# One DMA transpose moved behind the repeat copies, filler matmuls on vacated row tiles, and two of the last stores on the GpSimd queue

## The chip, the cores and the metric

The kernel runs on one core of a Trainium2 chip. The metric is the device time in microseconds (us) of one execution; a group of unprofiled runs is summed up by its median. One further execution was recorded by the hardware profiler, and all rows shown come from that execution. The engines are TensorE (PE in the rows, with its weight loads as PEld), VectorE (DVE), ScalarE (ACT), GpSimd (POOL) and SyncE (SP). DMA transfers are issued from the queues of SP, ACT and POOL.

## The reference, cut to what matters

Two layers follow each other: an attention over 32 inducing points, and a feed-forward layer with a parametric ReLU.

```
x: (4, 12480, 128)   inducing: (32, 128)   w_in: (128, 2048)   w_out: (2048, 128)   alpha: (2048)

mab(q, kv) = softmax(q @ kv.T / sqrt(128)) @ kv
h   = mab(inducing, x)                 # (4, 32, 128): one small summary for each batch
a   = mab(x, h)                        # (4, 12480, 128)
y   = a.reshape(49920, 128) @ w_in     # (49920, 2048)
g   = max(y, 0) + alpha * min(y, 0)
out = g @ w_out                        # (49920, 128), float32
```

Since `a` is a softmax over 32 rows of `h`, the kernel never forms it: `y` is the 32 exponentials of a token times the small matrix `h @ w_in` (32 x 2048), and the softmax's division is left to the very end. With g = relu(y) * (1 - alpha) + alpha * y, the second term is linear and also becomes a 32 x 128 matrix.

## The kernel before, in words

**Work units.** A batch has 12480 tokens: six supers of 2048 tokens (index `u` or `s` from 0 to 5) and a remainder of 192 tokens (index 6, `NS`). A super has four groups of 512 tokens, so a batch has groups `g` = 0 to 24, of which 24 is the remainder. A group's hidden layer has 16 chunks of 128 features (`KC`).

**First pass of a batch, over x.** `a_load` (line 170) loads a super of x through the POOL queue, cast to bf16, into `xn`. `a_xpose` (line 188) makes its transpose `xT` by one DMA transpose on the SP queue. `t_scores` and `t_accum` (lines 403, 417) or, for later batches, `a_scores` and `a_accum` then add to the summary `h`. This pass of batch `b + 1` runs during the second pass of batch `b`. In the second batch (batch 1) the supers 0 and 1 are transposed on PE, and the remainder and the supers 2 to 5 by DMA.

**Second pass of a batch, over its groups.** For each super `b_scores` (487) makes the exponentials `e` and writes them to DRAM scratch `e2d`; `b_rep` (511) reads them back four times, once into each quarter of the partitions, with four DMAs on the SP queue: the tile `rep`. `b_den` and `b_turn` (534, 552) write the reciprocals of the softmax's sums to scratch `rt` and read them back four times as `rdT`, also on SP. "The weights' copies" in the change's name are these `rdT` and `rep` transfers: the softmax weights of a super, copied to four places.

Then for each group:

- `fill` (595): a 32-row matmul on one of PE's four row tiles (`f` = 0 to 3; rows 32f to 32f+31) from `rep` and `hW` into a PSUM bank, and a ReLU by ACT (line 613) or DVE (616) into `gt`;
- `piece` (620): a 32-row matmul of `gt` with the weights `W1`, added up in the group's own bank; all 16 chunks times four row tiles must be added;
- `finish` (652): a DVE transpose of the finished bank (663), a multiply by `rdT` on POOL (666), and four stores of a quarter each (680).

**The planner.** `tokens` (817) writes out the order of all instructions by hand with a modelled clock (`clk`). Most groups are "laned": a group does its 16 pieces on row tile 0, then its 16 pieces on tile 1, and so on (`moving`, `tile[f]`), so that up to four groups are on the array at once, one on each row tile. A matmul on a free tile is a `fill` of a chunk needed later. The three last groups of the last batch, 22, 23 and 24, are not laned: their chunks are filled during the laned stage, and after it each is added with 128-row matmuls (`linear_whole`, `whole`; the `tail` loop at line 1071). When the laned stage starts, tiles 2 and 3 have no group yet, and `warm` matmuls, whose result is not used, run there into banks taken for that purpose (`fresh`, lines 949, 993, 1036).

**Tasks.** `at(t, ...)` (844) ties other work to the start of the t-th laned group (`T0` = 9 is the first of them). Tasks with the same t run in the order in which `at` was called; those of the current batch's second pass are entered before those of the next batch's first pass. `cross` (878) holds the t at which each super of batch 1 is given to `a_xpose`, in the order 0, 1, remainder, 2, 3, 4, 5. At `T0 + 6` stand the `rt` and `e2d` writes of batch 0 and the transpose of super 4; at `T0 + 7` stand `b_turn` (four `rdT` reads) and `b_rep` (four `rep` reads); at `T0 + 8` the transpose of super 5, whose x load is a task of `T0 + 6`.

**Stores.** They go to the POOL queue, except for the last four groups (`ending`, line 677): group 21's four go to SP, and those of groups 22 to 24 alternate between SP and ACT. Each DMA of the SP and ACT queues is given one of eight completion semaphores in turn, and its issue waits until the former DMA with that semaphore has landed; the POOL queue has eight of its own.

Of the kernel before, what the change touches and what calls it, by code (L numbers as in the profile page):

```python
# [41 lines left out]
def kernel(  # L42
# [9 lines left out]
    nc = tc.nc  # L52
# [3 lines left out]
    B, N, C = x.shape  # L56
# [8 lines left out]
    NG = NS * NQ + 1  # L65
# [7 lines left out]
    def pin(bi):  # L73
        ins = bi.ins
        e = ins.engine
        if e in last:
            tc.add_manual_dep(
                ins,
                last[e],
                mybir.DependencyInfo(  # L80
                    mybir.DependencyClass.NoSync, mybir.DependencyReason.DATA
                ),
                reason="program order",
            )
        last[e] = ins.name
        return bi
# [20 lines left out]
    number = {id(t): i for i, t in enumerate(banks)}  # L107
# [6 lines left out]
    clk = Clock()  # L114
    idle = list(range(NBANK - 2))

    def bank():
        i = min(idle, key=lambda i: clk.free[i])
        idle.remove(i)
        clk.pe = max(clk.pe, clk.free[i])  # L120
        return banks[i]
# [251 lines left out]
    def h_sum(st):  # L373
        st.et = work.tile([P, 1], f32, name="et", tag="et")
        pin(nc.vector.reduce_sum(out=st.et[:], in_=st.es[:], axis=AXX))
# [186 lines left out]
    def shape_of(g):  # L562
        return (P, NB, 1) if g < NS * NQ else (PR, JR, 2)
# [4 lines left out]
    begun = set()  # L568
    seen = {}
    held = []  # L570

    def units(g):
        return KC // shape_of(g)[2]

    def acc_of(b, g):
        if (b, g) not in accs:
            accs[b, g] = bank()
            left[b, g] = 4 * units(g) + 1
        return accs[b, g]
# [72 lines left out]
    def finish(b, g):  # L652
        st = states[b]
        pp, nb, _ = shape_of(g)
        t = pp * nb
        acc = acc_of(b, g)
        s, q = divmod(g, NQ)
        rq = st.rden[s][:, :, :, q : q + 1]
        rbc = bass.AP(
            tensor=rq.tensor, offset=rq.offset, ap=[rq.ap[0], rq.ap[1], rq.ap[2], [0, 32]]  # L660
        )
        ot = ot_pool.tile([P, GRP], f32, name="ot", tag="ot")
        pin(nc.vector.transpose(out=ot[:, :t], in_=acc[:, :t]))  # L663
        drained(accs[b, g], "D", 74 + t * 1.04)
        ob = ob_pool.tile([P, GRP], f32, name="ob", tag="ob")
        pin(nc.gpsimd.tensor_tensor(  # L666
            out=ob[:, :t].rearrange("p (k m c) -> p k m c", k=nb, c=32),
            in0=ot[:, :t].rearrange("p (k m c) -> p k m c", k=nb, c=32),
            in1=rbc, op=MULT,
        ))  # L670
        t0 = b * N + s * SUP
        if s < NS:
            dst = out[t0 : t0 + SUP, :].rearrange(
                "(i b q) (a k) -> q a i b k", b=t // 32, q=NQ, k=32)[q]
        else:
            dst = out[t0 : t0 + REM, :].rearrange("(i b) (a k) -> a i b k", b=t // 32, k=32)
        ending = b == B - 1 and g >= NG - 4
        for a in range(4):
            eng = (nc.sync, nc.scalar)[a % 2] if ending and g >= NG - 3 else nc.sync if ending else nc.gpsimd
            pin(eng.dma_start(  # L680
                out=dst[a],
                in_=ob[32 * a : 32 * a + 32, :t].rearrange("p (b k) -> p b k", k=32),
            ))
        st.rep.pop(g)

    order = [0, 1, NS] + list(range(2, NS))
# [3 lines left out]
    src = x[0, 0:SUP, :].rearrange("(p q j) c -> p q (j c)", q=NQ, j=NB)  # L690
# [27 lines left out]
    for q in range(4):  # L718
        sl = slice(32 * q, 32 * q + 32)
        pin(nc.gpsimd.memset(pick[sl, q : q + 1], 1.0))  # L720
        for q2 in range(4):
            pin(nc.gpsimd.tensor_copy(
                out=fold[sl, 32 * q2 : 32 * q2 + 32], in_=ident32[sl, sl]
# [93 lines left out]
    def tokens(st):  # L817
# [17 lines left out]
        need = [((first[y], 1, u), (*y, u)) for y in laned for u in range(KC)]  # L835
        need += [((c, 0, i), ch) for c, w in enumerate(wholes) for i, ch in enumerate(w)]
        need += [((len(laned) + i, 0, u), (*y, u)) for i, y in enumerate(tail) for u in range(units(y[1]))]
        need = [ch for _, ch in sorted(need)]
        SESSIONS = 8
        T0 = SESSIONS + 1  # L840
# [17 lines left out]
        for b in range(B):  # L858
            base = T0 + (first[b, 0] if b else -2)
            for s in range(1, NS + 1):  # L860
                t = base + 4 * s - AHEAD if b or s > 2 else 4 * s - 2
                nt = t + 4 if s < NS else t + 2
                at(t, lambda b=b, s=s: b_scores(states[b], s))
                at(t + 1, lambda b=b, s=s: b_rep(states[b], s))
                at(nt, lambda b=b, s=s: b_den(states[b], s))
                at(nt + 1, lambda b=b, s=s: b_turn(states[b], s))
            if b + 1 < B:
                n = b + 1
                E = base + 4 * NS
                if b:  # L870
                    lag = (-8, -4, -4, 0, 4, 8, 10) if b > 1 else (-4, 0, 0, 4, 6, 8, 10)
                    score = [base + k for k in lag]
                    load = [t - 7 for t in score]
                    cross = [t - 5 for t in score]
                else:
                    score = [T0 + k for k in (2, 4, 4, 6, 9, 11, 13)]
                    load = [0, 0, 5, SESSIONS, T0 + 2, T0 + 4, T0 + 6]
                    cross = [None, None, 6, T0 + 1, T0 + 4, T0 + 6, T0 + 8]
                    at(7, lambda: p_xpose(states[1], 0, 0))
                    at(SESSIONS, lambda: p_xpose(states[1], 0, 1))  # L880
                    at(T0 + 2, lambda: p_xpose(states[1], 1, 0))
                    at(T0 + 3, lambda: p_xpose(states[1], 1, 1))
                sums = [T0 + k for k in (4, 6, 6, 9, 11, 13, 14)] if n == 1 else [k + 4 for k in score]
                fs, fa = (t_scores, t_accum) if n == 1 else (a_scores, a_accum)
                for u, k, c, t, e in zip(order, score, cross, load, sums):
                    at(e, lambda n=n, u=u, fa=fa: fa(states[n], u))
                    at(k, lambda n=n, u=u, fs=fs: fs(states[n], u))
                    if c is not None:
                        at(c, lambda n=n, u=u: a_xpose(states[n], u))
                    at(t, lambda n=n, u=u: a_load(states[n], u, pieces=NQ if n > 1 else 2))  # L890
                H = sums[-1]
                if n == 1:
                    at(H + 1, lambda n=n: h_make(states[n]))
                    H += 2
                else:
                    at(score[-1] + 1, lambda n=n: h_sum(states[n]))
                    at(H, lambda n=n: h_den(states[n]))
                    at(H + 1, lambda n=n: h_transpose(states[n]))
                    H += 2
                assert H <= E - 6  # L900
                at(H, lambda n=n: h_weights(states[n]))
                at(H, lambda n=n: b_scores(states[n], 0))
                at(H, lambda n=n: h_linear(states[n]))
                at(H + 1, lambda n=n: b_rep(states[n], 0))
                at(E - 4, lambda n=n: b_den(states[n], 0))
                at(E - 3, lambda n=n: b_turn(states[n], 0))
                fn = lambda n=n: states.setdefault(n, new_batch(n))
                tasks.setdefault(load[0], []).insert(0, fn)
# [31 lines left out]
        queue = list(laned)  # L940
        tile = [None] * 4
        moving = []
        free_at = [clk.pe] * 4
# [5 lines left out]
        fresh = {f: bank() for f in (2, 3)}  # L949
# [10 lines left out]
        while queue or moving or any(tile):  # L960
            best = []
            taken = {q for _, q, _ in moving}
            for f in range(4):
                if tile[f]:
# [3 lines left out]
                    elif (*y, todo[0]) in seen:  # L968
                        t = max(free_at[f], seen[*y, todo[0]][1] - 100)
                        best.append((t, 1, f, "piece"))  # L970
                else:
# [4 lines left out]
                    if f == 0 and queue and lanes < LANES and (  # L976
# [3 lines left out]
                        if ch in seen:  # L980
                            t = max(free_at[f], seen[ch][1] - 100 - SLOT)
                            best.append((t, 2, f, "start"))
            if fillable():
                since = max(min(clk.free[i] for i in idle) - 40, landed.get(need[0][:2], 0))
                hungry = min(clk.act, clk.dve) < clk.pe + hungry_at
                for f in range(4):
                    t = max(free_at[f], since)
# [5 lines left out]
            for f in sorted(fresh):  # L993
                if soon and f not in taken:
                    best.append((free_at[f], 9, f, "warm"))
            assert best, (need[:2], len(seen), tile, moving, queue[:2])
            if closed:
                calm = [x for x in best if x[3] == "piece" and x[2] and x[2] not in gate]
                calm += [x for x in best if x[3] == "warm"]
                best = calm or [x for x in best if x[3] == "piece"] or best  # L1000
# [9 lines left out]
            if what == "start":  # L1010
                m = first[queue[0]]
                if pause(T0 + m):
# [8 lines left out]
                    free_at = [clk.pe] * 4  # L1021
# [4 lines left out]
            if what == "enter":  # L1026
# [4 lines left out]
                if f in fresh:  # L1031
                    i = number[id(fresh.pop(f))]
                    clk.free[i] = clk.pe + SLOT
                    idle.append(i)
                continue
            if what == "warm":
                mm(
                    fresh[f][:], W1[rows, 0, :],
                    W1[rows, 0:NB, :].rearrange("p k c -> p (k c)"), skip_group_check=True,
                )  # L1040
                free_at[f] = clk.pe + SLOT
                continue
# [23 lines left out]
                        flush()  # L1066
            free_at[f] = clk.pe + SLOT
        clk.pe = max(clk.pe, max(free_at) + SWITCH)
        for t in sorted(tasks):
            run_tasks(t)  # L1070
        for y in tail:
# [43 lines left out]
```

## Time and profile before

| | us |
|---|---|
| unprofiled runs | 563.68, 565.47, 568.73 (median 565.47) |
| the profiled execution | 570.99 |
| its span, from the first to the last instruction | 569.2 |
| mean granted TensorE clock in it | 0.988 of full speed |
| busy in the span: PE, ACT, DVE, POOL | 546.6, 505.3, 500.4, 408.7 |
| DMA queues' share of 16 engines: POOL's, SP's | 36.4%, 26.8% |
| longest idle time of PE after its start | 3.26 (from 88.66 to 91.93) |

The span is what the rows describe; the profiled execution's own time is 1.8 us longer. Times within the span are counted from its start. PE's busy time counts any moment at which at least one row tile works, so 96% does not mean that all four row tiles work.

### The profile page before, as it was taken

To read this page: it belongs to the slowest core of one execution; us is meant where nothing else is said; L and a number is where in the kernel's file an instruction comes from. 1 tells how busy PE (TensorE), PEld (TensorE's weight loads), DVE (VectorE), ACT (ScalarE), POOL (GpSimd) and SP (SyncE) were. 2 spreads that over 40 slices of the span, in tenths; PEclk is the share of its full clock that TensorE was granted. 3 is DMA by queue.
4 is the path that set the end of the run, shared out by engine and by line. 5 is a ranking of instruction groups with operands and counts; after the bars stand their busy time and mean duration, and the time that the engine had idled before them with its cause. 6 is when DMAs were issued, how large, how long until landed. Compare 5 with 4: busy or idle time off the path is not lost.

```text
span 569.2 us, 21360 instructions
## 1 busy us (share of the span) xinstructions
PE 546.6 (96%) x8860; PEld 295.4 (52%) x8864; DVE 500.4 (88%) x861; ACT 505.3 (89%) x1005; POOL 408.7 (72%) x600
## 2 busy tenths in 40 slices
PE   4999997999999999999999999999999999999995
PEld 4645553455455454454555565455555454474642
DVE  3689995899998999999999999999989999999971
ACT  2479995998999999999999999999999999999970
POOL 6646574676688997785987976865778777668681
PEclk9999997999999999999999999999999999999988
DMA  9976999555599997866796894333344244243233
GB/s 198 225 145 125 144 168 157 101 119 82 108 190 159 165 170 142 149 129 107 138 176 123 161 181 115 77 89 68 86 95 113 59 105 102 54 97 66 53 62 62
DMA packets 111201, 69.25 MB, mean 122 GB/s; under 512 B 79824, under 2 KB 101696, under 8 KB 111104
## 3 DMA queue, kind: packets, MB, share of 16 engines
q0 software_dynamic: 23280, 38.53, 36.4%
q1 hardware_dynamic: 85152, 28.52, 26.8%
q8 instruction: 69, 1.13, 0.9%
q10 hardware_dynamic: 2672, 0.84, 0.6%
q14 instruction: 28, 0.23, 0.1%
HBM read 41.00 MB, written 28.95 MB: 123 GB/s over the span
## 4 chain that ended last, share of the span: by engine, by line
POOL 35%; PE 32%; issue 20%; PEld 5%; DVE 4%; DMA 2%; POOLq 0%; SPq 0%; PEldq 0%; ACT 0%; DVEq 0%
PE bank L135 30%; POOL out_dram L680 23%; POOL ob L666 11%; PEld L135 5%; DVE gt L616 2%; PE bank L223 2%; POOL xn L177 1%; DMA ind_f<-in_inducing_dram 1%; DMA rep<-e2d 1%; DVE ot L663 1%; DVE hW L310 1%; DMA out_dram<-ob 0%; DVE xT L229 0%; POOLq L666 0%; PEldq L1061 0%
## 5 line engine op out<-in xcount | busy, mean ns | idle before, releaser
L135 PE MATMUL bank<-gt,W 32*128 32x512 bf16 (+2 forms) x6013 | 490.7, 376 | 4.3 <-issue 3.6
L613 ACT ACTIVATE gt<-bank 128x512 bf16<-128x512 f32 (+1 forms) x920 | 470.2, 615 | 23.9 <-PE bank L135 19.6
L616 DVE TENSOR_SCALAR gt<-bank 128x512 bf16<-128x512 f32 (+1 forms) x648 | 406.6, 677 | 26.8 <-PE bank L135 22.7
L135 PE MATMUL bank<-rep,hW 32*128 32x512 bf16 (+1 forms) x1600 | 415.5, 370 | 2.4 <-DVE hW L310 0.3
L135 PEld LDWEIGHTS <-W 32*128 32x128 bf16 (+1 forms) x6079 | 228.9, 92 | 188.5 <-issue 114.6
L680 POOL DMA_DIRECT2D out_dram<-ob x384 | 246.2, 672 | 43.0 <-POOL ob L666 28.9
L666 POOL TENSOR_TENSOR ob<-ot,rdT 128x512 f32<-128x512 f32 (+1 forms) x100 | 109.4, 1094 | 100.4 <-DVE ot L663 88.8
L135 PEld LDWEIGHTS <-hW 32*128 32x128 bf16 x1600 | 134.0, 92 | 36.7 <-issue 18.6
L663 DVE STREAM_TRANSPOSE ot<-bank 128x512 f32<-128x512 f32 (+1 forms) x100 | 69.7, 698 | 19.0 <-PE bank L135 18.0
L177 POOL DMA_DIRECT2D xn<-in_x_dram x70 | 40.2, 648 | 4.6 <-DMA xn<-in_x_dram 2.4
L135 PE MATMUL bank<-rep,hA 32*128 32x512 bf16 x94 | 35.3, 379 | 0.3 <-DVE hW L310 0.3
L229 DVE COPY xT<-bank 128x1024 bf16<-128x1024 bf16 (+1 forms) x16 | 10.7, 672 | 4.7 <-PE bank L223 4.6
L250 ACT ACTIVATE e1t<-bank 128x256 bf16<-128x256 f32 (+1 forms) x13 | 4.8, 371 | 9.9 <-PE bank L135 8.7
L135 PEld LDWEIGHTS <-hA 32*128 32x128 bf16 x94 | 8.5, 91 | 7.1 <-issue 5.3
L223 PE MATMUL bank<-ident,xn 128*128 128x128 bf16 x128 | 11.3, 242 | 0.9 <-DVE xn L781 0.9
L135 PE MATMUL bank<-xT,hT 128*32 128x512 bf16 (+1 forms) x98 | 10.4, 389 | 0.4 <-ACT gt L613 0.4
L135 PE MATMUL bank<-W 32*128 32x512 bf16 x63 | 10.3, 376 | 0.0
L498 ACT ACTIVATE e<-bank,rs 128x512 bf16<-128x512 f32 x12 | 8.5, 708 | 1.8 <-PE bank L135 1.7
L223 PEld LDWEIGHTS <-xn 128*128 128x128 bf16 x128 | 8.7, 109 | 2.1 <-DVE xn L781 1.0
L498 ACT ACTIVATE e<-bank 128x512 bf16<-128x512 f32 x12 | 7.5, 626 | 1.9 <-PE bank L135 1.8
L135 PE MATMUL bank<-IT,xT 128*128 128x32 bf16 x192 | 8.0, 179 | 0.6 <-issue 0.4
L135 PEld LDWEIGHTS <-e 128*128 128x128 bf16 x96 | 4.3, 96 | 7.4 <-issue 7.4
(100 smaller groups left out, 145.4 us busy)
## 6 DMA issues: line engine op xcount, KB each, us to landing
out_dram<-ob POOLq DMA_DIRECT2D x372, 64.0 KB, 2.7
rep<-e2d SPq DMA_DIRECT2D x92, 128.0 KB, 3.6
xn<-in_x_dram POOLq DMA_DIRECT2D x48, 128.0 KB, 5.8
xn<-in_x_dram POOLq DMA_DIRECT2D x22, 256.0 KB, 7.4
e2d<-e SPq DMA_DIRECT2D x24, 128.0 KB, 2.9
rdT<-rt SPq DMA_DIRECT2D x96, 8.0 KB, 2.2
w_out_f<-in_moe_w_out_dram POOLq DMA_DIRECT2D x4, 256.0 KB, 11.1
xs<-in_x_dram SPq DMA_DIRECT2D x1, 512.0 KB, 5.0
```

Source lines behind the costliest of these rows:

```text
L135: return pin(nc.tensor.matmul(o, lhsT, rhs, start=start, stop=stop, **kw))
L177: pin(nc.gpsimd.dma_start(out=xn[:, i * w : (i + 1) * w, :], in_=src[:, i * w : (i + 1) * w, :]))
L223: pin(nc.tensor.transpose(tp[:, k * P : (k + 1) * P], xn[:, q, j * C : (j + 1) * C], ident[:]))
L229: pin(nc.vector.tensor_copy(out=dst, in_=tp[:, :w]))
L250: pin(nc.scalar.activation(out=e1t[:pp, :nb, :].rearrange("p k m -> p (k m)"), in_=ps[:pp, : nb * M], func=EXP, scale=scale,))
L310: pin(nc.vector.tensor_scalar(out=out, in0=in_, scalar1=st.rs[:, 0:1], scalar2=1.0 / scale, op0=MULT, op1=MULT,))
L498: pin(nc.scalar.activation(out=e2[:].rearrange("p (t j i) -> p t j i", j=n, i=32), in_=turned(ps[:pp, :w], n), func=EXP, scale=scale_of(st ...
L613: pin(nc.scalar.activation(out=gt[:, :w], in_=ps[:, :w], func=RELU))
L616: pin(nc.vector.tensor_relu(gt[:, :w], ps[:, :w]))
L663: pin(nc.vector.transpose(out=ot[:, :t], in_=acc[:, :t]))
L666: pin(nc.gpsimd.tensor_tensor(out=ob[:, :t].rearrange("p (k m c) -> p k m c", k=nb, c=32), in0=ot[:, :t].rearrange("p (k m c) -> p k m c", ...
L680: pin(eng.dma_start(out=dst[a], in_=ob[32 * a : 32 * a + 32, :t].rearrange("p (b k) -> p b k", k=32),))
```

## The change

The task of super 4's transpose moves from `T0 + 6` to `T0 + 7`, where it comes after the `rdT` and `rep` copies. At the end of the laned stage, when no group is left to start and nothing is left to fill, row tiles below the lowest one that still has a group run `spare` matmuls: the same instruction as `warm`, into banks of their own, with a result that is not used. For group 23 the stores of quarters 2 and 3 are held back and issued on the POOL queue after group 24's multiply and stores.

```diff
@@ finish
         for a in range(4):
             eng = (nc.sync, nc.scalar)[a % 2] if ending and g >= NG - 3 else nc.sync if ending else nc.gpsimd
-            pin(eng.dma_start(
-                out=dst[a],
-                in_=ob[32 * a : 32 * a + 32, :t].rearrange("p (b k) -> p b k", k=32),
-            ))
+            src = ob[32 * a : 32 * a + 32, :t].rearrange("p (b k) -> p b k", k=32)
+            if b == B - 1 and g == NG - 2 and a > 1:
+                late.append((dst[a], src))
+            else:
+                pin(eng.dma_start(out=dst[a], in_=src))
+        if b == B - 1 and g == NG - 1:
+            for dst, src in late:
+                pin(nc.gpsimd.dma_start(out=dst, in_=src))
@@ tokens, tasks of batch 1
-                    cross = [None, None, 6, T0 + 1, T0 + 4, T0 + 6, T0 + 8]
+                    cross = [None, None, 6, T0 + 1, T0 + 4, T0 + 7, T0 + 8]
@@ tokens, the laned stage
+            if not queue and not need:
+                low = min([f for f in range(4) if tile[f]] + sorted(taken), default=4)
+                for f in range(low):
+                    best.append((free_at[f], 9, f, "spare"))
...
-            if what == "warm":
+            if what == "spare" and f not in fresh:
+                fresh[f] = bank()
+            if what in ("warm", "spare"):
                 mm(
                     fresh[f][:], W1[rows, 0, :],
                     W1[rows, 0:NB, :].rearrange("p k c -> p (k c)"), skip_group_check=True,
...
         clk.pe = max(clk.pe, max(free_at) + SWITCH)
+        for f in sorted(fresh):
+            i = number[id(fresh.pop(f))]
+            clk.free[i] = clk.pe
+            idle.append(i)
```

In the changed program's order of instructions, PE has 19 spare matmuls, all between the last fill and the last piece of group 21; SP and ACT have one store fewer each, POOL has two more; DVE's and ACT's ReLUs keep their order. In the first part nothing but the place of the one DMA transpose differs: it stands behind four `rdT` and four `rep` transfers and directly ahead of super 5's transpose.

More of the change, by code (lines that the diff above doesn't have):

```diff
@@ L570 @@
     held = []
+    late = []
     def units(g):
```

## The prediction

> **What bounds the kernel now.** I read the page's slices first, for places where PE or its clock gives way.
>
> ```profile
> PE   4999997999999999999999999999999999999995
> PEclk9999997999999999999999999999999999999988
> ```
>
> PE works in nearly every slice (one is 14.2 us). Between 98 and 548 us no idle gap of PE is over 0.42 us, and ACT and DVE are close behind it, so PE time lost before that stretch moves the end by as much. Two places stand out: slice 7 (85 to 100 us) and the last two, where the clock is down as well. The change touches both. The windows view, in steps of about 3.4 us around them (columns: stretch, its length, busy PE, PEld, DVE, ACT, POOL with counts, granted clock, DMA share, GB/s):
>
> ```profile
> 87.50:90.90 3.40, 1.16 (x20) 0.52 (x17) 1.77 (x3) 1.84 (x4) 0.48 (x1) 1.00 1.00 140
> 90.90:94.30 3.40, 2.37 (x23) 1.00 (x23) 0.69 (x1) 0.60 (x1) 0.76 (x2) 0.50 0.94 247
> 94.30:97.80 3.50, 3.50 (x35) 1.87 (x34) 2.00 (x3) 2.38 (x5) 1.43 (x2) 0.51 0.90 173
> 97.80:101.20 3.40, 3.40 (x80) 1.93 (x77) 2.88 (x6) 2.81 (x6) 2.20 (x4) 1.00 0.38 77
> ...
> 548.30:551.70 3.40, 3.38 (x33) 1.49 (x31) 2.81 (x6) 3.07 (x8) 2.76 (x5) 1.00 0.39 82
> 551.70:555.10 3.40, 3.18 (x9) 1.05 (x9) 0.72 (x1) 0.00 (x0) 3.31 (x5) 0.50 0.38 77
> 555.10:558.50 3.40, 3.40 (x17) 1.57 (x16) 0.72 (x1) 0.00 (x0) 0.14 (x1) 0.99 0.35 60
> ```
>
> The reader is to see: PE stands still around 90, then runs at half clock until 97.8 (35 matmuls in a stretch that holds 80 at full clock); and at 551.7 the clock falls to half once more, just as the unlaned groups 22 to 24 begin.
>
> *The first place.* The chain of waits has this piece:
>
> ```profile
> 88.66 3.26 issue
> ```
>
> No semaphore holds PE in it: the matmul that starts after it waits for nothing. What is missing is code. The page's "instruction" queue moved 69 packets, one for each 257 of PE's 17,724 records; it is PE's program. I compared the starts of these packets with the number of PE records begun by then. A packet is usually fetched 0.2 to 1 us after PE crosses into the one before; under heavy transfers it comes 2.9 to 4.9 us late (at 23, 63 and 78 us under a DMA transpose); the one that PE would have asked for at 79.75 starts at 89.12, when the records of the packet in hand (256, about 8 us of work) were used up. The DMA view of 79 to 89 us shows what went ahead of it, and the SP timeline who issued that:
>
> ```profile
> q1 hardware_dynamic: 2125, 0.58, 74.4%
> q0 software_dynamic: 209, 0.40, 56.5%
> ...
> rep<-e2d SPq DMA_DIRECT2D x3, 128.0 KB, 10.8
> rdT<-rt SPq DMA_DIRECT2D x4, 8.0 KB, 11.5
> ```
>
> ```profile
> 76.58 0.34 SPq L506 DMA_DIRECT2D e2d<-e  x1
> 77.01 4.36 SPq L191 DMA_TRANSPOSE xT<-xn  x1
> 81.46 1.95 SPq L559 DMA_DIRECT2D rdT<-rt  x4
> 83.52 8.53 SPq L516 DMA_DIRECT2D rep<-e2d  x4
> 93.04 2.44 SPq L191 DMA_TRANSPOSE xT<-xn  x1
> ```
>
> The transpose of super 4, issued at 77.0, lands at 91.7 by its semaphore. It shares the engines with the x load of super 5 (issued 77.4 to 79, landed 90.1 and 92.0). Behind it on SP's queue, `rep` and `rdT` take 10.8 and 11.5 us to land against 3.6 and 2.2 over the page, and the last `rep` waits until 91.75 because its semaphore is the transpose's. The next transpose, which runs with no x load beside it, lands in 4.6 us.
>
> *The second place.* The waits of SP's queue from 560 to 569 us, and its timeline:
>
> ```profile
> SPq L680 <- DMA out_dram<-ob: 1.2, 1, 1.2
> ```
>
> ```profile
> 565.68 1.26 SPq L680 DMA_DIRECT2D out_dram<-ob  x2
> ```
>
> These are group 24's two stores on SP. Its multiply ended at 563.58; the first store waits 1.2 us (of 1.9 from the issue before it) until the landing at 565.62 of group 23's ACT store, whose semaphore it shares. The second, issued at 566.30, lands last of all, at 568.24; the span ends 1.0 later.
>
> **The transpose moved.** It removes nothing. After the write of `e2d` has landed (81.5) the queue holds four `rdT`, four `rep`, then supers 4 and 5 back to back. `rdT` goes out from about 81, `rep` from 83 to 85; they land by 88 instead of 95.6, and PE first needs this `rep` later than that. The x load of super 5 meets only the end of super 3's transpose (landed 80.9), so the code packet asked for at 79.75 should come by 82, far ahead of 88.1. POOL, held by that x load's semaphores at 86.7 and 91.0 (3.7 and 1.2 us), goes free too. What is late next: super 4's transpose goes from 77 to 85, super 5's follows it, and both are first used by the scores of `T0 + 11` and `T0 + 13`, 109 us and after. Two at 4.6 end near 94. SP has nothing else to issue until 105.
>
> What it saves in this execution: from the matmul at 88.29 to that at 91.93 there are 3.6 us of standstill; then 5.83 us at half clock cost 2.9: together 6.5. By the records of PE's code, the 256 of that packet took 12.7 us against 7.7 on average later: 5.0. The gain for the profiled execution lies between 5.0 and 6.5.
>
> The Trainium skill, DMA: Bandwidth & Descriptors, section "Queues, rings and completion order", says that a DMA engine alternates packet by packet between the queues that have work; by that rule the code packet would not wait behind a whole transpose, and this term would be nothing, as in the first rival. The 9.4 us of its delay speak against reading it so here.
>
> How much of this is in the median run? The profiled execution is 570.99, 5.5 above the median, as much as the stall is worth: the median run may have none of it. Or the 5.5 has other causes, and it has all. Bounds 0 and 6.5; no row separates them, so I take the middle, 3.2.
>
> **The spare matmuls.** 19 are added (19 x 512 columns on 32 rows). They lie on tiles without work and beside group 21's last seven pieces, which already go at 0.216 us each, as four abreast do at 86 us. Not free: the second spare's bank is read last by an ACT ReLU that ends at 550.61, so the piece queued behind it goes at 550.65 instead of 550.34: +0.3, and DVE and POOL, which wait for group 21, have 1.5 us of other stores to issue meanwhile.
>
> What they may buy is the clock. The rows show it change only on a grid of 3.413 us. I added up, per grid window, columns times rows as a share of the full array: the window 548.32 to 551.73 has 0.34 and half clock follows; 87.52 to 90.93 has 0.22, likewise; every window that stayed at full clock has 0.48 or more. The spares add 19 x 0.053 = 1.0 us, 0.3 of a window, which brings the low window to 0.55 or more. At half clock seven 128-row matmuls went at 0.427 instead of 0.216: 1.5 us on the path PE, DVE transpose, POOL multiply, store. Net -1.2; +0.3 where the clock would not have fallen anyway. Where the grid lies differs from run to run: sliding the window over the records, the share is under 0.41 for edges from 550.5 to 552.6, 2.1 of 3.4 us. Six runs in ten have the loss; I take -1.2, bounds -1.5 and +0.3.
>
> The Trainium skill, TensorE: Matmul & The Clock Gate, Part 1, gives the same window (4096 cycles at 1.2 GHz, 3413 ns, free-running) and has the clock fall after an idle window. By that, filler beside a PE that is never idle for 0.5 us buys nothing, and this term would be +0.3, as in the last rival; the window at 0.34 shows a fall without idleness.
>
> **The stores.** SP now has one store of group 23 and two of 24, ACT one and two, POOL two. By the changed order of semaphores none of the last three on SP or ACT shares one with a transfer that lands after 562.8, so the 1.2 us wait is gone. On the old clock: group 24's multiply ends at 563.58; SP issues at 563.74 and 564.35, and the second lands 1.95 later, 566.3; ACT's last likewise; POOL begins 0.29 after its multiply, at 563.87, its second at 564.5 lands in the queue's usual 2.2: 566.7. Against 568.24 this is -1.5. POOL's own closing work (1.2 us past its last instruction) ends before that. Bounds: -1.9 (POOL lands as SP) to 0 (a landing of 2.8 and a POOL issue of 0.7 each, the longest rows, and a dearer close).
>
> **Sum.** Profiled execution: 570.99 - 5.0 - 1.2 - 1.5 = 563.3. Median run: 565.47 - 3.2 - 1.2 - 1.5 = 559.6.
>
> **Rivals.**
> - *The median run never had the stall.* Speaks for it: 570.99 against 565.47. Against: 568.73 among the runs. 565.47 - 2.7 = 562.8.
> - *The median run has all of it.* For: the order of SP's queue is the same in every run, and packets are late at three other transposes. 565.47 - 2.7 - 6.5 = 556.3.
> - *Two transposes back to back starve the next code packet.* PE asks for it at 88.1 and, no longer stalled, has used up what it holds by about 95.8. The pair starts at 85. At 4.6 each it is over at 94.2, 1.6 us before; at the 10.2 that super 4's took from the landing before it (81.5 to 91.7) at 105. It decides from a pair longer than 10.8 us. Price at the long end: 7 us of standstill and 2.9 of half clock; against a median run that had no stall, 565.47 - 2.7 + 9.9 = 572.7. Against it: the x load that slowed super 4 is over by then, only stores remain beside the pair.
> - *The change does not do what it says at the end:* the spares hold PE and the clock falls all the same, and POOL's landing is the last. 565.47 + 0.3, less the 3.2: 562.6; it ends beside the first rival.
>
> **Chances.** Forecast 0.44 (own range 557.5 to 562), no stall or nothing from the end 0.24, whole stall 0.21, starved packet 0.11. What a measurement of this kernel can tell from no change is about 1%, here 559.8 and 571.1. The whole stall and a little over half of the forecast are faster: 0.46. Slower takes most of the starved packet: 0.10. The rest, 0.44, is within. The range leaves out the starved packet and the edges: 555.8 to 566.5.
>
> **What would show it.** In the new profile: no "issue" piece near 88, `rep` landing in 4 to 6 us there, slice 7 of PEclk at 9; then PE busy through 94 to 97. A new "issue" piece at about 96 would be the starved packet. At the end: full clock from 548 to 560, matmuls of 0.216 from the first of group 22 on, PE's end 1.2 earlier, no wait of SP for a store, last landing on POOL's queue, 2.5 to 3 us earlier. I am wrong if the stall is gone and the span is not 4 us shorter, or if half clock appears at 551 in spite of the spares.

## The result, and the profile after

The changed kernel takes 562.05 us (median of 9 runs, 561.6 to 562.34). The kernel before, run beside it, took 568.58 (median of 9, 563.68 to 573.54). The ratio is 0.9906, 95% interval 0.9877 to 0.9935. It leaves out runs over 1.5% above the fastest of their kernel, which here takes away the longest run of the kernel before (573.54), so it is nearer to 1 than the two medians are. 0.9% is just inside the 1% or so that the prediction took as what a measurement of this kernel can tell from no change. The fastest runs differ by only 2 us; what the change took away is mostly spread. In three later sets the kernel before gave 565.74 and 567.66 (35 runs each, 562.5 to 574.8) and 567.92 (23 runs, 562.5 to 575.1).

The profiled execution took 562.34 us, with a span of 560.5 and a granted clock of 0.998 (before 570.99, 569.2, 0.988). In its slices PE and its clock no longer give way at either place:

```profile
PE   4999999999999999999999999999999999999995
PEclk9999999999999999999999999999999999999999
```

The windows view of the first place, in the stretches shown of before (stretch, length, busy PE, PEld, DVE, ACT, POOL with counts, clock, DMA share, GB/s):

```profile
87.50:90.90 3.40, 3.40 (x62) 2.16 (x62) 3.32 (x7) 3.35 (x7) 0.66 (x2) 1.00 1.18 124
90.90:94.30 3.40, 3.40 (x80) 2.13 (x77) 3.12 (x6) 2.96 (x7) 2.53 (x4) 1.00 1.29 154
94.30:97.80 3.50, 3.50 (x65) 1.50 (x58) 3.41 (x6) 3.47 (x8) 2.74 (x4) 1.00 0.75 182
```

PE is busy all through, at full clock, where it stood still and then ran at half clock. The SP timeline (start, duration of the issues and their waits) and the DMA view of 79 to 89 us say why:

```profile
81.09 2.86 SPq L559 DMA_DIRECT2D rdT<-rt  x4
84.06 1.79 SPq L516 DMA_DIRECT2D rep<-e2d  x4
85.96 8.21 SPq L191 DMA_TRANSPOSE xT<-xn  x2
```

```profile
rep<-e2d SPq DMA_DIRECT2D x4, 128.0 KB, 3.5
rdT<-rt SPq DMA_DIRECT2D x4, 8.0 KB, 4.3
```

The copies land in 3.5 and 4.3 us instead of 10.8 and 11.5. PE's code packet, asked for at 79.78, is fetched at 82.60, a delay of 2.8 us instead of 9.4. The two transposes follow; the first has landed at 94.7 and the second at 96.9.

At the end the clock holds. The windows, 6.8 us earlier than those of before, since the work comes 6.6 earlier:

```profile
541.50:544.90 3.40, 3.37 (x46) 1.46 (x46) 2.98 (x6) 3.24 (x8) 2.76 (x5) 1.00 0.39 82
544.90:548.30 3.40, 3.35 (x25) 1.45 (x19) 0.72 (x1) 0.00 (x0) 3.40 (x5) 1.00 0.38 77
548.30:551.70 3.40, 3.40 (x18) 1.51 (x16) 0.72 (x1) 0.00 (x0) 1.17 (x2) 1.00 0.33 58
```

The middle stretch holds 25 matmuls instead of 9. The waits of SP's queue (551 to 560.5 us) no longer contain a store waiting for a landing; what is left is the wait for the multiply:

```profile
SPq L685 <- POOL ob L667: 3.1, 2, 2.9
```

But the 24 KB stores land more slowly (DMA view of 553 to 560 us; last column: median us from issue to landing):

```profile
out_dram<-ob POOLq DMA_DIRECT2D x2, 64.0 KB, 2.6
...
out_dram<-ob SPq DMA_DIRECT2D x2, 24.0 KB, 2.6
out_dram<-ob ACTq DMA_DIRECT2D x2, 24.0 KB, 2.7
```

The same view of the kernel before, 565.3 to 569 us:

```profile
out_dram<-ob ACTq DMA_DIRECT2D x2, 24.0 KB, 1.9
```

The last landing is ACT's, at 559.32; POOL's is at 558.88.

### The profile page after: what moved, and what is told of

It is laid out like the page before. It is cut to its first block, busy times and chain, and to the rows that moved or that the text cites. A ratio compares the mean times of both kernels' runs of the same rounds, so it can differ in the third digit from the quotient of the medians.

```text
span 560.5 us, 21396 instructions
## 1 busy us (share of the span) xinstructions
PE 542.5 (97%) x8879; PEld 294.9 (53%) x8883; DVE 499.7 (89%) x861; ACT 504.6 (90%) x1005; POOL 411.1 (73%) x602
## 4 chain that ended last, share of the span: by engine, by line
PE 67%; issue 10%; PEld 9%; DMA 4%; DVE 4%; POOL 3%; ACT 1%; SPq 0%; PEldq 0%; POOLq 0%; DVEq 0%
PE bank L135 67%; PEld L135 9%; DMA xn<-in_x_dram 3%; DVE gt L617 2%; ACT gt L614 1%; POOL out_dram L685 1%; DVE ot L664 1%; POOL xn L177 1%; POOL ob L667 1%; DMA rt<-rd 1%; DVE hW L310 1%; PE bank L223 0%; SPq L559 0%; DMA rdT<-rt 0%; PEldq L1072 0%
## 5 line engine op out<-in xcount | busy, mean ns | idle before, releaser
L229 DVE COPY xT<-bank 128x1024 bf16<-128x1024 bf16 (+1 forms) x16 | 10.8, 672 | 5.3 <-PE bank L223 5.0
L135 PE MATMUL bank<-W 32*128 32x512 bf16 x82 | 12.2, 376 | 0.0
```

Of the source, the lines that this page charges most:

```text
L135: return pin(nc.tensor.matmul(o, lhsT, rhs, start=start, stop=stop, **kw))
L229: pin(nc.vector.tensor_copy(out=dst, in_=tp[:, :w]))
```

## The experiments

Two theories stood against each other. Mine: PE stands still because a packet of its own code comes late whenever a DMA transpose and an x load run together. The rival: what costs is the place of the transpose on SP's queue, ahead of `rdT` and `rep`. Each kernel below ran 12 times, and one execution of each was profiled; "clock" is the mean granted clock of a run. The starts of code packets are set against the count of PE's records, as in the prediction; by that count PE stops 0.5 to 1 us after a packet has run out.

### The parts, one at a time

**The move alone**, on the kernel before:

```diff
-                    cross = [None, None, 6, T0 + 1, T0 + 4, T0 + 6, T0 + 8]
+                    cross = [None, None, 6, T0 + 1, T0 + 4, T0 + 7, T0 + 8]
```

> The kernel before with only super 4's transpose moved behind the copies (no spare matmuls, old stores). Theory (the late code packet makes the stall, and the move removes it in every run): no standstill of PE near 88 us and no half clock until 98; runs between 562.5 and 564.8 us, so all of the long runs of before (up to 573) are gone, median about 564.2 = 562.05 + 1.3 for the clock at the end + 0.8 for the stores. Rival (the long runs come from the end of the kernel, or from something the move does not touch): median within 2 us of before's 568.6, with runs over 567.

Measured: 562.63 (562.12 to 565.26), ratio 0.9959 (0.9927 to 0.9991), beside 565.74 for the kernel before. No standstill near 88; the last fill begins at 543.21, in the changed kernel at 543.37. The theory holds, but the median is 1.6 below the 564.2 expected. Seven runs lie at 562.12 to 562.64 with a clock of 0.996 or 0.997, five at 563.65 to 565.26 with 0.993 or 0.994. Their clock and their 2 us more fit one step of 3.41 us at half clock; none of the five was profiled, so where it fell was not seen.

**The changed kernel without the spares:**

```diff
-            if not queue and not need:
+            if False:
```

> The changed kernel without the 19 spare matmuls. Theory (a window of the clock's 3.413 us grid with too little array work halves the clock, although PE is never idle): two sorts of runs by where the grid lies, some 6 in 10 at about 563.4 us (1.64 lost to half clock, 0.32 saved since no piece waits behind a spare) and the others at about 561.7. Rival by the rule of an idle window: the clock does not fall at the end in any run, all at about 561.7, 0.3 faster than the changed kernel.

Measured: 562.13 (561.61 to 564.21). Ten runs are at 561.61 to 562.60, as good as the changed kernel; two, with a clock of 0.994, at 563.64 and 564.21: two in twelve, where six in ten were expected. In its profile the last fill and group 21's hand-over (the first 128-row matmul of group 22) begin 1.94 us apart, against 2.27 with the spares: they cost 0.33.

**The changed kernel with all of group 23's stores on SP and ACT again:**

```diff
-            if b == B - 1 and g == NG - 2 and a > 1:
+            if False:
```

> The changed kernel with group 23's four stores back on SP and ACT. Theory (the two stores on POOL save 0.8 us by the two traces: 8.7 less in the span, 7.9 of it already there at group 24's multiply): 562.9 us, 0.8 slower than the changed kernel. My prediction's term of 1.5: 563.5. Rival (only the shared completion semaphore cost time, and it falls elsewhere in this order): no difference, 562.0.

Measured: 562.14 (561.59 to 563.09), clock 0.997 or more in all runs: the rival's 562.0 was nearer than the 562.9 expected. From the end of group 24's multiply to the span's end it takes 4.94 us, against 4.86 in the changed kernel and 5.67 with the move alone. So POOL's queue itself brings about 0.1. The wait of SP for a landing, 1.2 with the move alone, is only 0.6 here:

```profile
SPq L685 <- DMA out_dram<-ob: 0.6, 1, 0.6
```

Group 24's four stores go out in another order than with the move alone, and their semaphores fall elsewhere; SP's last store is issued 0.7 earlier after the multiply (2.00 instead of 2.72). Why the spares change that order was not tried.

**The changed kernel with the transpose at its old place** (the first diff in reverse):

> The changed kernel with super 4's transpose back at its old place; spares and new stores kept. Theory: the wide spread of the kernel before comes back, runs from about 561.9 to 571 us, median near 566.5 (before's 568.6 less 2.1 for the end), and the profile has an issue gap of PE between 85 and 92 us in the long ones. Rival (the end makes the difference): 562 to 563.5 us with little spread.

Measured: 565.12 (561.49 to 570.48), ratio 0.9992 (0.995 to 1.0035). Most of the spread is back (beside it the kernel before goes up to 574.26). The profiled execution has the old standstill in its chain of waits, and a longer one:

```profile
88.44 4.77 issue
```

The packet asked for at 80.24 was fetched 10.55 us later. Spares and stores do nothing for this; the move removes it alone. It does not explain all of the kernel before: one such standstill (6.5) and one fall of the clock (1.6) on top of the shortest run, 562.5, make 570.6, and no run above 571 was profiled.

### Is it the code packet?

**The kernel before with 64 useless matmuls ahead of PE's first instruction,** where PE waits anyway. Nothing is moved; only the packets' borders lie elsewhere in the work.

```diff
+    pad = bank()
+    for _ in range(64):
+        mm(pad[:32, :32], ident[:, :32], ident[:, :32])
+    drained(pad, "D", 0, 0)
     ps = bank()
     itp = ps[:].bitcast(bf16)
```

> The kernel before, with 64 useless 32-column matmuls on PE ahead of its first instruction (PE waits there until 6.45 us anyway), and nothing else. They are 128 records of PE's program, half a code packet, so every later packet is asked for about half a packet earlier in the work: by the records of before, the one that was asked for at 79.75 and ran out at 88.13 becomes one asked for at 76.5, which runs out at 84.0, and one asked for at 84.0, which runs out at about 92. The order on SP's and POOL's queues is as before, so rep and rdT still land in about 11 us. Theory (PE stands still because its code packet is fetched late, behind transpose and x load): the first is fetched by 78 to 81, the second by 89 to 91.7, both in time; no issue piece near 88 or 92, and the runs lie close together at 562 to 563, with some at 564 to 565 where the clock falls at the end, like the kernel with the move alone (562.63). Rival (PE stands still because rep and rdT, or something behind them, come late): the standstill stays near 88.7 and the runs spread from 562.5 to 574, median 565 or so, as before.

Measured: 564.97 (562.83 to 568.72), beside 567.66 for the kernel before; ratio 0.9996 (0.9962 to 1.003). My expectation of tight runs failed, and the reason speaks for the theory. The standstill near 88 is gone, with SP's order untouched, but there is one earlier:

```profile
76.97 2.02 issue
```

The packet whose records run out at 75.92 had been asked for at 68.63, just after the transpose of super 3 (issued 68.14) had met the x load of super 4 (issued 66.46 to 67.7), and was fetched at 76.14. Every kernel here has this meeting. In the others the packet is asked for late in it, at about 73, and is fetched 2 to 3 us before it is needed (in the kernel before at 77.85 for 79.75). I had only followed the packets at 76.5 and 84. The useless matmuls change nothing about the copies on SP's queue up to there, so the rival has no reason for a standstill at 77. That there is none near 88 fits as well, though it says less, since PE's pause had shifted the work. Super 4's transpose (issued 78.03, landed 89.05) and the x load of super 5 (issued from 81.8) still met, but PE asked for a packet late in that meeting, at about 86.4; it was fetched at 89.63 and not needed before 94.5.

**The kernel before with the x load of super 5 later,** and the transpose of super 4 still ahead of the copies:

```diff
-                    load = [0, 0, 5, SESSIONS, T0 + 2, T0 + 4, T0 + 6]
-                    cross = [None, None, 6, T0 + 1, T0 + 4, T0 + 6, T0 + 8]
+                    load = [0, 0, 5, SESSIONS, T0 + 2, T0 + 4, T0 + 8]
+                    cross = [None, None, 6, T0 + 1, T0 + 4, T0 + 6, T0 + 9]
```

> The kernel before, with the x load of super 5 at T0 + 8 instead of T0 + 6 (its transpose at T0 + 9 instead of T0 + 8, since it needs the load). Super 4's transpose stays ahead of the rdT and rep copies on SP's queue. Theory (a transpose beside the x load holds back PE's code): alone, super 4's transpose lands in 4.6 to 6 us, by 83, the code packet asked for near 79.8 is fetched by 84, rep lands in 4 to 6 us; no standstill near 88, runs at 562 to 563 with some at 564 to 565. The code packet asked for at about 88 now meets the x load, but no transpose; it has until 94.5. Rival (the place of the transpose ahead of the copies on SP's queue is what costs): standstill and spread as before, median 565 or so.

Measured: 564.19 (561.76 to 570.15), ratio 0.9961 (0.9919 to 1.0002). Its profile has no standstill; the packet asked for at 79.31 is fetched at 81.03; and the copies behind the transpose land fast (DMA view of 78 to 88 us):

```profile
rep<-e2d SPq DMA_DIRECT2D x4, 128.0 KB, 2.8
rdT<-rt SPq DMA_DIRECT2D x4, 8.0 KB, 3.2
```

The order on SP's queue is not what costs. Eleven runs are at 561.76 to 565.23, and seven of these have a clock of 0.992 to 0.994. The profiled one is among the seven and lost time to the clock at the end. Windows of it:

```profile
540.70:544.10 3.40, 3.40 (x32) 1.42 (x31) 2.72 (x6) 2.98 (x7) 3.11 (x5) 1.00 0.39 82
544.10:547.50 3.40, 3.40 (x10) 1.19 (x9) 0.72 (x1) 0.00 (x0) 3.40 (x5) 0.50 0.38 77
```

PE is busy for 3.40 of 3.40 us, but with columns times rows at only 0.33 of the full array, little more than one of four row tiles on average (32 matmuls, some of them short; 80 fit where four row tiles work at full clock), and the clock falls all the same. The run at 570.15 is too long for this; what it lost was not seen.

**The changed kernel with the x load beside the moved pair:**

```diff
-                    load = [0, 0, 5, SESSIONS, T0 + 2, T0 + 4, T0 + 6]
+                    load = [0, 0, 5, SESSIONS, T0 + 2, T0 + 4, T0 + 7]
```

> The kernel after, with the x load of super 5 at T0 + 7 instead of T0 + 6, so that it runs beside the moved transposes instead of ahead of them. Theory (a transpose beside the x load holds back PE's code, wherever the two meet): the transpose of super 4 takes 8 to 10 us again, and the code packet that PE asks for at 88.0 comes near or after 94.5, when the one in hand is used up; in the profile its delay grows from 4.1 us to 6 or more, and in some runs there is a standstill near 95, then half clock: median 562 to 566 with a spread of several us. Rival (the order on SP's queue alone decides): no standstill, median 562.0 within 0.5, clock 0.997 or more in all runs.

Measured: 564.06 (561.77 to 568.89), ratio 0.9982 (0.9949 to 1.0015). The two transposes now take 15.6 us to land in the median (DMA view of 86 to 97 us; below it that of 85 to 96 us of the changed kernel, with 8.0), and the chain of waits has a standstill at the next packet:

```profile
xT<-xn SPq DMA_TRANSPOSE x2, 15.6
```

```profile
xT<-xn SPq DMA_TRANSPOSE x2, 8.0
```

```profile
95.42 5.00 issue
```

This packet was asked for at 88.35, its forerunner ran out at 94.85, and it was fetched at 97.67. The copies on SP's queue were as early as in the changed kernel. So in every profile with a standstill the late packet was asked for early in a meeting of a transpose and an x load, wherever that was, and the profiles without a standstill have no packet of that kind. The pair without an x load delays the packet too, but less: it was fetched 4.1 us after it was asked for in the changed kernel, 2.4 with the move alone. An x load without a transpose stands beside a packet only in the kernel with the later load, and shows little there: the packet asked for at about 87.2 was fetched at 88.33, while the load was still being issued (87.27 to 88.5). Which of the two holds it on the DMA engines, and by what rule, these runs don't show.

### Fewer spares

**The changed kernel with spares only from the point where fewer than six pieces are left,** 15 instead of 19; none of them is queued behind the ReLU that ends last:

```diff
-            if not queue and not need:
+            if not queue and not need and min([len(tile[f][1]) for f in range(4) if tile[f]], default=9) < 6:
```

> The kernel after, with the spare matmuls only from the point where fewer than six pieces are left to the last lane: 15 spares instead of 19, and none of those queued ahead of a piece behind the ACT ReLU that ends last. Theory: the 0.33 us that the spares cost between the last fill and the hand-over of group 21 goes to 0.1 or less, and the 15 that are left still put 0.23 of a clock window into the low one (0.34 becomes 0.57, above the 0.41 that was seen to stay at full clock); so median 561.7 to 561.8 with all clocks at 0.997 or more. Rival (the wait was not the bank's, or the earlier spares are needed for the clock): median 562.0 or more, or some runs at 564 with a clock of 0.994.

Measured: 561.58 (561.07 to 562.62), clock 0.997 or more in all runs; last fill to hand-over 1.94 us, the price of the spares gone. The clock's steps of 3.41 us have an edge at 542.28; the windows around it:

```profile
538.90:542.30 3.40, 3.38 (x43) 1.32 (x39) 3.40 (x7) 3.40 (x9) 2.75 (x5) 1.00 0.29 60
542.30:545.70 3.40, 3.40 (x40) 1.95 (x38) 2.39 (x5) 2.06 (x6) 3.10 (x6) 1.00 0.26 55
```

Full clock in both; the second holds 40 matmuls, where the step that stands there with the move alone holds 23, with columns times rows at 0.41 of the full array. That one keeps the clock too, as the step behind it shows:

```profile
542.55:545.96 3.41, 3.36 (x23) 1.43 (x23) 2.40 (x5) 2.03 (x6) 3.12 (x5) 1.00 0.27 57
545.96:549.40 3.44, 3.44 (x18) 1.57 (x16) 0.35 (x2) 0.00 (x0) 2.28 (x3) 1.00 0.29 60
```

Since the changed kernel had been measured on another occasion, both ran once more side by side.

> The kernel after once more, on the same chip as the one with fewer spares, so that the two can be set side by side. Theory (the first spares cost 0.33 us between the last fill and the hand-over of group 21): 562.0 to 562.1, as before, which is 0.4 to 0.5 above the kernel with 15 spares. Rival (the 0.47 between 562.05 and 561.58 is the difference of two chips): the two medians are within 0.15 of each other.

> The kernel with 15 spares instead of 19, once more, on the same chip as the kernel after. Theory: 561.6, 0.4 to 0.5 below the kernel after, of which 0.33 are the wait; clock 0.997 or more in all runs. Rival: the two medians are within 0.15 of each other.

Measured: 562.39 (561.64 to 564.51) for the changed kernel, 561.80 (561.20 to 562.27) for the one with 15 spares; against the kernel before, 0.9936 (0.9904 to 0.9969) and 0.9914 (0.9882 to 0.9946). The medians differ by 0.59 here and by 0.47 across the earlier sets; the profiles show 0.33 of it (2.28 against 1.95 us from last fill to hand-over). The version with 15 spares is the best of those run, though the two intervals overlap.

## Why the prediction was right, and where it was wrong

Its mechanism holds in the profiled execution, with a change in each of the three terms the way it was forecast: 563.3 forecast, 562.34 measured. Its range, 555.8 to 566.5, holds the median. But the median was put at 559.6 and came out at 562.05, just outside the forecast's own 557.5 to 562, and that step was wrong.

| term, profiled execution | forecast | measured, and from what |
|---|---|---|
| transpose moved | -5.0 (to -6.5) | -6.6: start of the last fill, 550.00 to 543.37 |
| spares | -1.2 | -1.3: last fill to the end of group 24's multiply, 13.58 to 12.30 |
| stores | -1.5 | -0.8: from there to the span's end, 5.63 to 4.86 |
| sum | -7.7 | -8.7 |

**The move.** The cause was right: the code packet, late where the transpose runs together with the x load. (The copies behind them are late too, but the kernel with the later x load shows that their place is not the cost.) Of my two values for its worth, the count from the standstill and the matmuls at half clock (6.5) was right and the one from the records (5.0) too low: it took the 256 records of that packet at the average of later packets, 7.7 us, but in the changed kernel the records asked for at the same point take 6.5 (88.03 to 94.53).

**The median.** The step that failed is the sum 565.47 - 3.2 - 1.2 - 1.5: the middle of "bounds 0 and 6.5" is taken off a median run, and the whole of the end's -2.7 besides. The two sums contradicted each other: a profiled execution rid of stall and clock fall comes to 563.3, and a median run can't be 3.7 faster than one that has neither. The kernel before has runs at 562.5 that lost nothing; less what the end still gives there (+0.3 and -0.8), that is 562.0. The first rival's 562.8 and the fourth's 562.6 were nearer, though for other reasons: the first has no standstill in the median run, the fourth gets nothing from the end. By the runs the mis-sized part is the end: against the set beside it the move alone took the median from 565.74 to 562.63, 3.1, close to the middle, which was a guess; spares and stores together brought only 0.6 more in the median (562.63 to 562.05), not 2.7. And it is luck that the median's change came near the forecast, -6.5 against -5.9: the base was 565.47 from three runs where nine gave 568.58, and the result is too low by nearly as much. From 565.74 the whole change is 3.7.

**The spares.** Both parts were well sized: the wait 0.33 for 0.3, the clock 1.57 for 1.5 (from the hand-over to PE's last matmul it takes 10.24 us in the profile with the later x load, 8.67 with the move alone). How often was too high: of 36 runs of the three kernels without spares and without the old meeting (move alone, no spares, later x load), 14 (five, two and seven of twelve) have a clock of 0.992 to 0.994 and lie about 2 us above the others of their kernel, as one fall of the clock would make it: four in ten instead of six; with spares, of the 48 runs of the four such kernels in this count (old stores, changed kernel again, 15 spares twice), none. In a run whose clock would have held they cost 0.33, as forecast. So they take away the longer runs and leave the median about where it is. The reason for six in ten was a limit put at 0.41 of the array, half-way between 0.34 and 0.48: the profile with the move alone has a window at 0.41 that keeps the clock, and the later load has one at 0.33 that loses it.

The Trainium skill, TensorE: Matmul & The Clock Gate, Part 1, has the clock fall after an idle window. The window 540.7 to 544.1 above, with PE busy for all of its 3.40 us, with columns times rows at 0.33 of the full array, shows that a fall doesn't need idleness.

**The stores.** Two causes, of which the first was a mis-sized term: I let the last stores land in the 1.95 us of before, but with three queues storing at once they took 2.6 to 2.7. The wait of 1.2 is gone, and 0.7 of it came back as slower landings. The last landing was ACT's, 3.65 after the multiply, not POOL's at 3.1. Then the span's close takes 1.21 after that landing instead of 0.97. And, by the kernel with the old stores, most of what is left comes from the order of the semaphores.

**The rival of the starved packet** did not decide in the changed kernel: the packet asked for at 88.03 was fetched at 92.17, 2.4 us before the one in hand ran out. But its condition was put wrongly. I had it decide from a pair longer than 10.8 us; the pair took 10.9, from 85.96 to 96.86 (two at 4.6 were forecast, ending near 94), and the packet came before either transpose had landed. It does not wait for the pair's end. The rival is real all the same: with the x load beside it the pair took 22.0 from the first issue to the last landing, and the profiled run was 568.89, 6.5 above the changed kernel's. Its price was not worked out right either: from 95.8 to 105 are 9.2 us of standstill, not 7.

## What to carry to other kernels

Before you add up what a change removes in the median, ask what a run that loses nothing takes: no sum may go below it, and the profiled execution corrected for all its losses should meet it. A standstill whose releaser is "issue" is worth a comparison with the starts of the code packets; here it helped to keep the DMA transpose and the bulk load apart at the moment when PE asks for a packet. Filler matmuls that protect the clock should start only where nothing useful queues behind them.

## What the runs showed of the hardware that was not expected

- From the start of a late code packet to PE's next matmul it takes about as long each time: 89.12 to 91.93, 76.14 to 78.99, 97.67 to 100.43 (2.8 us), and 90.78 to 93.21 (2.4). A standstill of 2 to 5 us was followed by half clock for one or two steps of 3.41 us in all four profiles that have one (6.83, 3.41, 3.41, 6.83).
- Half a packet more of code at the start moved the standstill by 12 us (88.66 to 76.97). So an edit that only adds or removes instructions on PE can move a standstill, because the packets' borders move in the work.
- With all three queues storing at once, 24 KB took 2.6 to 2.7 us to land (median of each queue, changed kernel); with SP and ACT alone 1.9 to 2.0 (kernel before, old stores).
